# Relu² attention and a PReLU feed-forward on one core: two score chunks, not three, behind each A@V, and a second plain run of three under FFN1

## The chip, the cores and the metric

The kernel runs on one core of a Trainium2 chip. The metric is the device time of one execution in microseconds (us). The profile is that of one execution; its engines are PE (TensorE's matmuls), PEld (TensorE's weight loads), DVE (VectorE), ACT (ScalarE), POOL (GpSimd) and SP (SyncE, which here only issues DMAs).

## The reference

```python
# q, k, v: (8 batches, 12 heads, 448 tokens, 64), float32
scores = scale * np.matmul(q, k.transpose(0, 1, 3, 2))      # scale = 1/sqrt(64)
attn = np.maximum(scores, 0.0) ** 2 / S                      # S = 448
attn_out = np.matmul(attn, v)
x = attn_out.transpose(0, 2, 1, 3).reshape(B * S, H * D)     # 3584 x 768
h = x @ w_in                                                 # w_in: 768 x 2048
g = np.maximum(h, 0.0) + alpha * np.minimum(h, 0.0)          # alpha: 2048
out = g @ w_out                                              # w_out: 2048 x 768
```

## The kernel before

The matmuls run in bf16. Four heads of one batch make a *group*; there are 8 x 3 = 24 groups, n = 0 to 23. The 448 tokens are cut into 7 slices of 64 keys, j = 0 to 6. One (group, slice) is a *chunk*: `score_mm` gives it a pair of PSUM banks and four matmuls on 64x64 tiles of the array, `relu` takes it out of PSUM (on ScalarE for "A", on DVE for "D"), and `square` multiplies it with itself on DVE into an `at` tile. When all seven `at` tiles of a group are there, `attnv(n)` runs 28 matmuls on 64x64 tiles, and its result goes, half by ScalarE (line 205) and half by DVE (line 206), into `xT`, the input of the feed-forward.

FFN1 of a batch is 16 calls `f1(b, ff)`: six full-array matmuls into one bank, then `neg` on ScalarE (line 237) and the step that writes `gT` on DVE (line 238). FFN2 works on two batches together: `f2(sb, c, hf)` is 16 matmuls for 128 tokens and half of the columns, a copy `osb` on ScalarE (line 254) and two stores from SP's queue (line 260). After FFN1 of an even batch come 6 such units, after an odd one 8.

Attention of the next batches is woven into this by hand. The order in the source is the order on every engine (`manual_schedule`). The 126 chunks of groups 6 to 23 stand in one list, and `some(k)` takes the next k of it, with engines "ADA". `run(some(3))` is a *plain run*: three chunks' scores, relus and squares. `burst(n)` is a *burst*: three chunks' scores, `attnv(n)`, three more chunks' scores, then all six squares. Before: plain runs after three of the first FFN2 units, bursts 6, 7 and 8, and then in every batch from 2 to 6 one plain run before ff 8 and three bursts between the FFN2 units. That is 3 + 3 x 6 = 21 chunks a batch, as many as three groups have.

PSUM's eight banks are handed out at build time by age: `take_pair` gives the aligned pair whose younger use is oldest, `take_bank` the oldest bank. A matmul then waits until whoever last read that bank is done.

Groups from 6 on are transposed by DMA. `prepare(n)` calls `turn_dma(n)`: two DVE copies into `perm` (line 155) and one DMA transpose from SP's queue into a T tile (line 157, four buffers), which `score_mm` reads. It then has POOL load q, k and v of group n + 2 (lines 91 and 98), which takes buffers that the copies have freed. In a batch with n0 = 3(b + 1), `prepare(n0 + 2)` stands before ff 8, `prepare(n0 + 3)` before `burst(n0)` and `prepare(n0 + 4)` before `burst(n0 + 2)`. Other buffers that matter: `rl` 7, `at` 12, `neg` 3, `osb` 4.

Of the kernel before, what the change touches and what calls it, by code (L numbers as in the profile page):

```python
# [20 lines left out]
def kernel(  # L21
# [56 lines left out]
    def take_bank():  # L78
        i = min(range(8), key=lambda i: (taken[i], i))
        take(i, 1)  # L80
        return psum[:, i]
# [82 lines left out]
    def score_mm(n, j):  # L164
        ps = take_pair()
        t = T[n]
        for r in range(2):
            for c in range(2):
                nc.tensor.matmul(ps[64 * c:64 * c + 64, r, :S],  # L169
                                 t[64 * r:64 * r + 64, 1, j, 64 * c:64 * c + 64],  # L170
                                 t[64 * r:64 * r + 64, 0, :, 64 * c:64 * c + 64],
                                 start=True, stop=True)
        return ps

    def relu(ps, eng):
        rl = rl_pool.tile([128, 2, S], BF16, tag="rl", name="rl")
        if eng == "A":
            nc.scalar.activation(rl, ps[:, :, :S], ACTF.Relu)  # L178
        else:
            nc.vector.tensor_scalar(rl, ps[:, :, :S], 0.0, None, ALU.max)  # L180
        return rl
# [6 lines left out]
    def attnv(n):  # L188
        ps = take_pair()
        vv = vraw.pop(n)  # L190
        for j in range(NJ):
            a = att.pop((n, j))
            for r in range(2):
                for s in range(2):
                    nc.tensor.matmul(ps[64 * s:64 * s + 64, r, :S],  # L195
                                     vv[64 * r:64 * r + 64, s, j, :],
                                     a[64 * r:64 * r + 64, s],
                                     start=(j == 0), stop=(j == NJ - 1))
        b, g = divmod(n, NG)
        if g == 0:  # L200
            xT[b] = xT_pool.tile([128, NG, 2, S], BF16, tag="xT", name="xT")
        if n < 2:
            nc.scalar.activation(xT[b][:, g], ps[:, :, :S], ACTF.Copy, scale=out_scale)
            return
        nc.scalar.activation(xT[b][:, g, 0], ps[:, 0, :S], ACTF.Copy, scale=out_scale)  # L205
        nc.vector.tensor_scalar(xT[b][:, g, 1], ps[:, 1, :S], out_scale, None, ALU.mult)  # L206
# [3 lines left out]
    def sc(chunks):  # L210

        for n, j, eng in chunks:
            late.append((n, j, relu(score_mm(n, j), eng)))

    def sq(k=99):
        for g in late[:k]:
            square(*g)
        del late[:k]

    def run(chunks):  # L220
        sc(chunks)
        sq()
# [19 lines left out]
    def f1(b, ff):  # L242
        ps = take_bank()[:, :S]
        f1_mm(ps, b, ff, range(KM))
        f1_out(ps, b, ff)

    def f2(sb, c, hf, parts=((0, HALF),)):
        o = o_pool.tile([128, HALF], F32, tag="o", name="osb")
        for lo, hi in parts:
            ps = take_bank()[:, :hi - lo]  # L250
            for ff in range(KF):
                nc.tensor.matmul(ps, gT[sb][:, ff, bass.ts(c, 128)], w_out_sb[:, hf, ff, lo:hi],  # L252
                                 start=(ff == 0), stop=(ff == KF - 1))
            nc.scalar.copy(o[:, lo:hi], ps)  # L254
            for u in range(2):
                blk = 2 * c + u
                b, j = 2 * sb + blk // NJ, blk % NJ
                rows = out[b * S:(b + 1) * S].rearrange("(pp j) d -> j pp d", j=NJ)
                eng = nc.scalar if u and hi - lo < HALF else nc.sync
                eng.dma_start(out=rows[j][:, hf * HALF + lo:hf * HALF + hi], in_=o[64 * u:64 * u + 64, lo:hi])  # L260
# [57 lines left out]
    def prepare(n):  # L318
        if n < NQ:
            turn_dma(n)  # L320
        if n + 2 < NQ:
            load_qk(n + 2)
            load_v(n + 2)
# [38 lines left out]
    def some(k):  # L362
        lo = at_c[0]
        at_c[0] = min(lo + k, len(chunks))
        return [(n, j, e) for (n, j), e in zip(chunks[lo:at_c[0]], "ADA")]

    def burst(n):

        sc(some(3))
        attnv(n)  # L370
        sc(some(3))
        sq()

    early = []
# [19 lines left out]
    f2(0, 1, 1)  # L394
    run(some(3))
    f2(0, 2, 1)
    f2(0, 4, 0)
    prepare(9)
    burst(6)
    f2(0, 4, 1)  # L400
    f2(0, 5, 0)
    burst(7)
    f2(0, 5, 1)
    f2(0, 6, 0)
    prepare(10)
    burst(8)
    f2(0, 6, 1)

    for b in range(2, B):
        n0 = NG * (b + 1)  # L410
        last = b == B - 1
        sb = b // 2
        for ff in range(KF):
            if not last and ff == 8:
                run(some(3))
                prepare(n0 + 2)
            f1(b, ff)
        if b % 2 == 0:
            units = [(sb, c, h) for c in range(3) for h in range(2)]
            at = {1: 0, 3: 1, 5: 2}  # L420
        else:
            units = [(sb, c, h) for c in range(3, 7) for h in range(2)]
            at = {1: 0, 4: 1, 7: 2}
        for i, u in enumerate(units):
            if i in at and not last:
                g = at[i]
                if g != 1:
                    prepare(n0 + 3 + g // 2)
                burst(n0 + g)
            if last and i == len(units) - 1:  # L430
                f2(*u, parts=((0, 256), (256, HALF)))
            else:
                f2(*u)
# [30 lines left out]
```

## Time and profile before

| | |
|---|---|
| five runs, us | 393.89, 399.61, 392.79, 398.99, 401.05 |
| median, us | 398.99 |
| the profiled execution's own time, us | 394.08 |
| its span, us | 392.3 |
| PE busy | 379.0 us, 97% of the span |
| DVE busy | 263.6 us, 67% |
| ACT busy | 207.5 us, 53% |
| TensorE clock granted | full, in all slices |

The span is the time from the first to the last instruction of the program. Busy times are sums over instructions. PE's matmuls are pipelined and their ends are modelled, so lengths of PE's entries overlap what follows; the distance from one start to the next is the better measure. A time of a trace line is counted from the span's start.

| stage, from the trace | PE's time, us from the span's start |
|---|---|
| FFN1 of batch 2 | 125.18 to 144.14 |
| FFN2 units and bursts behind it | 144.14 to 168.16 |
| FFN1 of batch 3 | 168.16 to 187.11 |
| FFN2 units and bursts behind it | 187.11 to 216.50 |
| FFN1 of batch 4 | 216.50 to 235.46 |
| FFN1 of batch 7, the last | 349.56 to 367.72 |

### The profile page before, as it was taken

To read this page: it belongs to the slowest core of one execution; us is meant where nothing else is said; L and a number is where in the kernel's file an instruction comes from. 1 tells how busy PE (TensorE), PEld (TensorE's weight loads), DVE (VectorE), ACT (ScalarE), POOL (GpSimd) and SP (SyncE) were. 2 spreads that over 40 slices of the span, in tenths; PEclk is the share of its full clock that TensorE was granted. 3 is DMA by queue.
4 is the path that set the end of the run, shared out by engine and by line. 5 is a ranking of instruction groups with operands and counts; after the bars stand their busy time and mean duration, and the time that the engine had idled before them with its cause. 6 is when DMAs were issued, how large, how long until landed. Compare 5 with 4: busy or idle time off the path is not lost.

```text
span 392.3 us, 7956 instructions
## 1 busy us (share of the span) xinstructions
PE 379.0 (97%) x3228; PEld 215.7 (55%) x3228; DVE 263.6 (67%) x418; ACT 207.5 (53%) x332; POOL 65.6 (17%) x97
## 2 busy tenths in 40 slices
PE   6779999989999999999999999999999999999996
PEld 5434454535666456654666556655565546655564
DVE  3977965845678687878756688778756786735400
ACT  4966565524655546645545455565544556524311
POOL 7558112520202021202202022011100000000000
PEclk9999999999999999999999999999999999999999
DMA  9999999999677279482957339490842302120033
GB/s 177 191 204 203 206 211 201 139 149 194 99 122 124 56 119 165 77 116 31 170 118 135 64 41 173 105 144 15 143 96 49 89 10 60 42 60 2 11 72 81
DMA packets 71909, 43.75 MB, mean 112 GB/s; under 512 B 38208, under 2 KB 71872, under 8 KB 71872
## 3 DMA queue, kind: packets, MB, share of 16 engines
q0 software_dynamic: 27312, 23.04, 41.1%
q1 hardware_dynamic: 44128, 19.65, 25.3%
q8 instruction: 25, 0.41, 0.5%
q10 hardware_dynamic: 432, 0.56, 0.4%
q14 instruction: 12, 0.10, 0.1%
HBM read 47.00 MB, written 11.01 MB: 148 GB/s over the span
## 4 chain that ended last, share of the span: by engine, by line
PE 84%; DVE 6%; ACT 4%; DMA 4%; issue 1%; ACTq 0%; DVEq 0%
PE psum L252 37%; PE psum L229 32%; PE psum L169 7%; PE psum L195 6%; ACT rl L178 3%; DMA T<-perm 3%; DVE at L185 2%; DVE gT L238 1%; DMA qfirst<-in_q_dram 1%; DVE T L147 1%; DVE rl L180 1%; PE psum L144 1%; ACT xT L205 1%; DVE perm L155 0%; ACT osb L254 0%
## 5 line engine op out<-in xcount | busy, mean ns | idle before, releaser
L252 PE MATMUL psum<-w_out_sb,gT 128*128 128x384 bf16 (+2 forms) x912 | 151.8, 323 | 1.8 <-DVE gT L238 1.6
L229 PE MATMUL psum<-xT,w_in_sb 128*128 128x448 bf16 x768 | 148.7, 353 | 1.1 <-ACT xT L205 0.6
L252 PEld LDWEIGHTS <-gT 128*128 128x128 bf16 x912 | 87.6, 98 | 64.3 <-issue 6.7
L229 PEld LDWEIGHTS <-w_in_sb 128*128 128x128 bf16 x768 | 74.2, 98 | 71.8 <-issue 4.4
L238 DVE SCALAR_TENSOR_TENSOR gT<-neg,beta_sb,psum 128x448 bf16<-128x448 f32 x128 | 84.2, 679 | 39.9 <-ACT neg L237 39.5
L237 ACT ACTIVATE neg<-psum 128x448 f32<-128x448 f32 x128 | 69.3, 545 | 73.4 <-PE psum L229 63.5
L178 ACT ACTIVATE rl<-psum 128x896 bf16<-128x896 f32 x120 | 102.9, 928 | 1.2 <-PE psum L169 1.2
L185 DVE TENSOR_TENSOR at<-rl 128x896 bf16<-128x896 bf16 x168 | 94.1, 620 | 3.5 <-ACT rl L178 3.4
L254 ACT COPY osb<-psum 128x384 f32<-128x384 f32 (+2 forms) x57 | 27.0, 474 | 97.0 <-PE psum L252 91.5
L180 DVE TENSOR_SCALAR rl<-psum 128x896 bf16<-128x896 f32 x48 | 52.2, 1087 | 36.2 <-PE psum L169 36.2
L91 POOL DMA_DIRECT2D qraw<-in_q_dram x24 | 17.2, 719 | 193.0 <-DVE perm L155 172.2
L169 PE MATMUL psum<-T 64*64 64x448 bf16 x672 | 44.7, 355 | 3.6 <-ACT rl L178 1.3
L195 PE MATMUL psum<-at,vraw 64*64 64x448 bf16 x672 | 37.9, 351 | 0.7 <-DVE at L185 0.3
L169 PEld LDWEIGHTS <-T 64*64 64x64 bf16 x672 | 20.9, 105 | 21.2 <-issue 14.5
L195 PEld LDWEIGHTS <-vraw 64*64 64x64 bf16 x672 | 24.8, 106 | 11.0 <-issue 3.4
L206 DVE TENSOR_SCALAR xT<-psum 128x448 bf16<-128x448 f32 x22 | 13.7, 625 | 14.3 <-PE psum L195 7.2
L91 POOL DMA_DIRECT2D kraw<-in_k_dram x24 | 17.5, 728 | 7.2 <-DMA w_out_sb<-in_moe_w_out_dram 3.4
L98 POOL DMA_DIRECT2D vraw<-in_v_dram x25 | 18.2, 730 | 1.2 <-DMA w_in_sb<-in_moe_w_in_dram 0.3
L155 DVE COPY perm<-qraw 128x896 bf16<-128x896 bf16 x18 | 11.1, 615 | 5.7 <-DMA T<-perm 5.7
L205 ACT ACTIVATE xT<-psum 128x448 bf16<-128x448 f32 x22 | 12.0, 545 | 5.4 <-PE psum L195 5.4
L108 POOL DMA_DIRECT2D w_in_sb<-in_moe_w_in_dram x16 | 10.0, 627 | 7.8 <-DMA vraw<-in_v_dram 2.5
L155 DVE COPY perm<-kraw 128x896 bf16<-128x896 bf16 x18 | 11.0, 611 | 0.0
(19 smaller groups left out, 34.6 us busy)
## 6 DMA issues: line engine op xcount, KB each, us to landing
out_dram<-osb SPq DMA_DIRECT2D x110, 96.0 KB, 3.0
vraw<-in_v_dram POOLq DMA_DIRECT2D x25, 224.0 KB, 7.6
qraw<-in_q_dram POOLq DMA_DIRECT2D x24, 224.0 KB, 5.2
kraw<-in_k_dram POOLq DMA_DIRECT2D x24, 224.0 KB, 6.9
w_in_sb<-in_moe_w_in_dram POOLq DMA_DIRECT2D x16, 192.0 KB, 8.5
w_out_sb<-in_moe_w_out_dram POOLq DMA_DIRECT2D x2, 1536.0 KB, 18.9
qfirst<-in_q_dram SPq DMA_DIRECT2D x1, 448.0 KB, 4.5
kfirst<-in_k_dram ACTq DMA_DIRECT2D x1, 448.0 KB, 4.8
```

Of the source, the lines that this page charges most:

```text
L91: nc.gpsimd.dma_start(out=t.rearrange("p m j d -> p m (j d)"), in_=flat[:, 2 * g:2 * g + 2])
L155: nc.vector.tensor_copy(p[:, i], raw.pop((n, name)).rearrange("p s j d -> p j s d"))
L169: nc.tensor.matmul(ps[64 * c:64 * c + 64, r, :S], t[64 * r:64 * r + 64, 1, j, 64 * c:64 * c + 64], t[64 * r:64 * r + 64, 0, :, 64 * c:64 * ...
L178: nc.scalar.activation(rl, ps[:, :, :S], ACTF.Relu)
L180: nc.vector.tensor_scalar(rl, ps[:, :, :S], 0.0, None, ALU.max)
L185: nc.vector.tensor_tensor(a, rl, rl, ALU.mult)
L195: nc.tensor.matmul(ps[64 * s:64 * s + 64, r, :S], vv[64 * r:64 * r + 64, s, j, :], a[64 * r:64 * r + 64, s], start=(j == 0), stop=(j == NJ ...
L229: nc.tensor.matmul(ps, w_in_sb[:, km // 2, km % 2, bass.ts(ff, 128)], xT[b][:, km // 2, km % 2, :], start=(km == 0), stop=(km == KM - 1))
L237: nc.scalar.activation(neg, ps, ACTF.Relu, scale=-1.0)
L238: nc.vector.scalar_tensor_tensor(gT[b // 2][:, ff, (b % 2) * S:(b % 2) * S + S], neg, beta_sb[:, ff:ff + 1], ps, ALU.mult, ALU.add)
L252: nc.tensor.matmul(ps, gT[sb][:, ff, bass.ts(c, 128)], w_out_sb[:, hf, ff, lo:hi], start=(ff == 0), stop=(ff == KF - 1))
L254: nc.scalar.copy(o[:, lo:hi], ps)
```

## The change

The second part of a burst takes two chunks in place of three, so that its squares are five. A fourth plain run stands in the first FFN2 units, before `f2(0, 4, 0)`. In batches 2 to 6 the plain run before ff 8 is taken out, and one stands before ff 5 and another before ff 11; `prepare(n0 + 2)` stays before ff 8. A batch has 2 x 3 + 3 x 5 = 21 chunks again.

```diff
@@ def burst(n)
         sc(some(3))
         attnv(n)
-        sc(some(3))
+        sc(some(2))
         sq()
...
     f2(0, 1, 1)
     run(some(3))
     f2(0, 2, 1)
+    run(some(3))
     f2(0, 4, 0)
     prepare(9)
     burst(6)
...
         for ff in range(KF):
+            if not last and ff in (5, 11):
+                run(some(3))
             if not last and ff == 8:
-                run(some(3))
                 prepare(n0 + 2)
             f1(b, ff)
```

## The prediction

> **What bounds the kernel now.** I read the page first: busy times, then the chain that ended last.
>
> ```profile
> PE 379.0 (97%) x3228; PEld 215.7 (55%) x3228; DVE 263.6 (67%) x418; ACT 207.5 (53%) x332; POOL 65.6 (17%) x97
> PE 84%; DVE 6%; ACT 4%; DMA 4%; issue 1%; ACTq 0%; DVEq 0%
> ```
>
> TensorE is busy in 97% of the span and makes 84% of the chain. DVE and ScalarE have room on average. Next the waits of PE: all together they are under 10 us, and nearly all lie before 89 us. The change acts from 98 us on, so it can gain only what hides inside PE's busy time. I therefore took PE's timeline, in which each line gives start, length, engine and operation, and measured from start to start. First a burst of batch 4 (three score chunks, the A@V, three score chunks, then FFN2), with ScalarE's xT copy of its A@V:
>
> ```profile
> 238.16 0.76 PE L169 MATMUL psum<-T 64*64 64x448 bf16 x12
> 238.75 1.56 PE L195 MATMUL psum<-at,vraw 64*64 64x448 bf16 x28
> 240.07 0.80 PE L169 MATMUL psum<-T 64*64 64x448 bf16 x12
> 240.28 0.54 ACT L205 ACTIVATE xT<-psum 128x448 bf16<-128x448 f32 x1
> 240.87 5.36 PE L252 MATMUL psum<-w_out_sb,gT 128*128 128x384 bf16 x32
> ```
>
> The burst takes 240.87 - 238.16 = 2.71 us. Its last three chunks take 0.80 until FFN2 starts. ScalarE's xT copy ends at 240.82, 0.05 before FFN2's first matmul: FFN2 is handed the A@V's bank and waits for it. Now the plain run of batch 4 under FFN1, and FFN1 of the last batch, which has none:
>
> ```profile
> 225.68 0.76 PE L169 MATMUL psum<-T 64*64 64x448 bf16 x12
> 226.37 9.25 PE L229 MATMUL psum<-xT,w_in_sb 128*128 128x448 bf16 x48
> 349.56 18.32 PE L229 MATMUL psum<-xT,w_in_sb 128*128 128x448 bf16 x96
> 367.72 21.00 PE L252 MATMUL psum<-w_out_sb,gT 128*128 128x384 bf16 x144
> ```
>
> FFN1 without a run: 367.72 - 349.56 = 18.16, or 1.135 for each ff. FFN1 of batch 4, with the run, goes from 216.50 to FFN2's start at 235.46: 18.96.
>
> **What is added: six plain runs of three chunks.** One goes before f2(0, 4, 0); in batches 2 to 6 the run before ff 8 becomes two, before ff 5 and ff 11. A run costs PE 18.96 - 18.16 = 0.80 us. The runs between FFN2 units say the same: FFN2 starts at 95.12 and 98.52 with a unit of 2.60 and a run between, 0.80. Six cost 4.80 us. Three chunks of matmuls are some 3 x 0.19 = 0.57 of each 0.80 (0.19 is the difference between a score part of 8 matmuls, 57.46 to 57.86, and one of 12, 0.59); the other 0.23 is for entering and leaving 64x64 tiles.
>
> [...]
>
> **What is removed: a chunk of each burst.** 17 bursts have a second part now (groups 6 to 22). Each loses a chunk; group 22 loses two, since the list of 126 chunks runs out there. 16 + 2 = 18 chunks, the same as six runs. The trace has one burst of the new shape already, before batch 2:
>
> ```profile
> 57.86 1.49 PE L195 MATMUL psum<-at,vraw 64*64 64x448 bf16 x28
> 59.18 0.55 PE L169 MATMUL psum<-T 64*64 64x448 bf16 x8
> 59.66 2.77 PE L252 MATMUL psum<-w_out_sb,gT 128*128 128x384 bf16 x16
> ```
>
> Two chunks after the A@V: FFN2 starts 0.48 later, not 0.80. I followed the oldest-bank rule of take_pair and take_bank through the new order: FFN2 then gets the pair of the burst's third chunk, not the A@V's. That chunk's relu, ScalarE's second of the burst, ends 2.21 us after the burst's start (238.64 + 1.73), and FFN2 would start at 1.91 + 0.48 = 2.39, so the xT copy leaves PE's path with 0.18 to spare. 13 bursts save 0.80 - 0.48 = 0.32 each (4.16); the later two of batches 3 and 5 have 0.82 there and save 0.34 (4 x 0.34 = 1.36); group 22's second chunk is 0.19. Total 5.71. Bound from below: if FFN2 waited elsewhere, only the work would go, 18 x 0.19 = 3.4. I take 5.71, since the row has the same shape.
>
> **What moves between ScalarE and DVE.** some() gives its chunks "ADA", so a part of two is A, D: one relu per batch goes from ScalarE (0.93) to DVE (1.09). Neither is on the path in FFN2.
>
> **DVE under FFN1.** What hides the work there is this row: DVE after the run of batch 4.
>
> ```profile
> 226.96 1.08 DVE L180 TENSOR_SCALAR rl<-psum 128x896 bf16<-128x896 f32 x1
> 227.96 1.69 DVE L185 TENSOR_TENSOR at<-rl 128x896 bf16<-128x896 bf16 x3
> 229.56 0.61 DVE L155 COPY perm<-qraw 128x896 bf16<-128x896 bf16 x1
> 230.09 0.61 DVE L155 COPY perm<-kraw 128x896 bf16<-128x896 bf16 x1
> 230.62 3.04 DVE L238 SCALAR_TENSOR_TENSOR gT<-neg,beta_sb,psum 128x448 bf16<-128x448 f32 x5
> ```
>
> A run costs DVE 1.0 + 1.6, the two perm copies 1.1, a gT step 0.61 when queued and 0.68 when not. From the first run to FFN1's end PE takes 11 x 1.135 + 2 x 0.80 = 14.1 us; DVE has 11 x 0.61 to 0.68 + 2 x 2.6 + 1.1 = 13.0 to 13.8. It just fits. Step by step from the first run's start: squares end at 3.9, gT of ff 5, 6, 7 at 5.7, perm at 6.9, gT of 8, 9 at 8.0, gT of 10 at 8.9, then the second run's relu and squares to 11.6. The second run begins at 7.6; f1 of ff 11 begins at 8.3 in the bank of ff 9 (released at 8.0, 0.2 to spare with the semaphore); ff 12 at 9.4 in that of ff 10 (0.5 to spare). gT of 15 ends near 15.4, and FFN2's first unit needs it only in its last matmul, near 16.4. Cost taken: nothing. Without that cover, one gT step (0.65) too late costs about 0.5 per batch, 2.5 in five. In the new run before f2(0, 4, 0) DVE is tight as well: perm of prepare(9) ends about 1.0 after burst 6 begins, its D relu at 2.1, just when the second part asks for its bank at 2.10. Cost 0 to 0.1.
>
> **The T tiles.** The lead in chunks at a batch's start stays 27, but inside a batch chunks are taken earlier, so T is read sooner after its DMA transpose. SP's order is as before: the transpose stands behind the two stores of the unit ahead of the burst, which wait for ScalarE's osb copy. In the rows it issues 1.82 after its burst starts:
>
> ```profile
> 239.98 2.07 SPq L157 DMA_TRANSPOSE T<-perm  x1
> 255.99 3.06 SPq L157 DMA_TRANSPOSE T<-perm  x1
> DMA to landing us min/median/max: 3.5/7.7/14.5
> ```
>
> Asked one by one, the first lands after 7.7, the second after 9.2. Three cases. The T prepared ahead of a batch's first burst is now read by the last chunk of the next burst (chunk 42 is the first of group 12): in batches 2 and 4 at 8.01 - 0.32 + 2.10 = 9.79 after the first burst's start, against landings at 1.82 + 7.8 = 9.62 and 1.82 + 7.7 = 9.52; group 9 ahead of burst 6: 9.82 against 1.87 + 7.4. Margins 0.2 to 0.6. The T prepared ahead of the third burst is read by the second chunk of the ff 5 run: 2.39 + 2.60 + 5 x 1.135 + 0.10 + 0.19 = 10.96, against 1.82 + 9.2 = 11.02 after batches 2 and 4: 0.1 late each. Batches 3 and 5 have 10.7 us between bursts and landings of 3.6 to 7.7, so they are safe. The T prepared at ff 8 gains, because its perm no longer stands behind a run (about 1.6 earlier): over 1 to spare. POOL's loads follow their perm copies as before. I take 0.2 for all this.
>
> **Sum.** 4.80 - 5.71 + 0.2 = -0.7 us. The profiled execution took 394.08 (span 392.3 and 1.8 around it), so its like would be 393.4. The median of the runs shown is 398.99, 4.9 higher, in a spread from 392.79 to 401.05; on that footing I predict 398.3. About 2% is what a measurement of this kernel can tell from no change.
>
> **Rivals.**
>
> *T comes late (slower).* Place: last chunk of the second burst in batches 2 and 4 and of burst 7. If those transposes land after 9.2, as two neighbours do, each is read 11.0 - 9.8 = 1.2 before it lands: 3 x 1.2 = 3.6, and the sum is +2.7: 396.8 like the profile, 401.7 at the median. It decides once the three are 0.3 late on average, at landings of about 8.3. For: 9.2, 8.8 and 8.3 stand in the trace. Against: these three measured 7.4 to 7.8 in the same surroundings. Over 2% it takes landings like the 11.8 to 14.5 at 71 to 85 us, when DMA was crowded.
>
> *DVE becomes FFN1's bound.* 2.5 as above, sum +1.8: 395.9, or 400.8. For: 0.2 to spare, and at 85 to 88 us PE did step with DVE's gT, at 0.59 for each matmul. Against: DVE idles 0.46 in each ff with no run near, and makes that up.
>
> *The bursts give back only their work*, because FFN2 waits for the third chunk's relu instead: 4.80 - 3.4 + 0.2 = +1.6, 395.7 or 400.6. For: only 0.18 to spare. Against: the row at 59 us.
>
> *Clearly faster.* Over 2% is 8 us. All of the bursts' time beyond matmul work is 17 x (2.71 - 13 x 0.19) = 4 us, so nothing in the profile can give it; only a change in the spread of runs could.
>
> **How the numbers follow.** Forecast 0.60 (own range on the profile's footing 392 to 395); T late 0.17; DVE 0.09; work only 0.10; clearly faster 0.04. Of the T and DVE cases 0.10 is put beyond 2%. Same: 0.60 + 0.10 + 0.16 = 0.86. The range takes the low footing less a little, 391.8, up to T late at the median and a bit more, 402.5.
>
> **What would show it.** Right: FFN1 of batches 2 to 6 at 19.8 (+0.80); burst to FFN2 near 2.39 with an 8-matmul second part; the xT copy no longer just ahead of FFN2; PE with no new waits above 0.2. Wrong: PE waiting at L169 for T by DMA in second bursts or in the ff 5 run; PE waiting at L229 for gT after the second run; FFN2 starting 0.05 after a relu of ScalarE.

## The result, and the profile after

The changed kernel is slower: 1.0091 times the time before, 95% interval 1.0069 to 1.0113, some 3.6 us on 392. Its median over 46 runs is 398.87 (393.58 to 409.24). The kernel before, with 86 runs by then, has a median of 393.45 (391.13 to 401.88). Both spread for a reason of their own, taken up below: a wait of PE near 85 us that one trace shows and another does not. The ratio compares the runs within 1.5% of each kernel's fastest; the profiled execution of the changed kernel, 403.82 (span 402.1), is not among them, so its stages are compared with those of before, and its total is not.

The page's busy times and chain:

```profile
PE 384.9 (96%) x3228; PEld 213.7 (53%) x3228; DVE 267.5 (67%) x423; ACT 203.2 (51%) x327; POOL 65.6 (16%) x97
PE 83%; DMA 7%; DVE 5%; ACT 3%; issue 1%; ACTq 0%; DVEq 0%
```

PE's two longest waits (total us, times, longest):

```profile
PE psum L252 <- DVE gT L238: 2.9, 4, 2.1
PE psum L169 <- DMA T<-perm: 2.6, 1, 2.6
```

DMA's share of the chain is 7%, up from 4%, and PE has a wait that it did not have: 2.6 us, once, for a T tile. PE's timeline shows it in burst 7:

```profile
116.96 0.76 PE L169 MATMUL psum<-T 64*64 64x448 bf16 x12
117.55 1.56 PE L195 MATMUL psum<-at,vraw 64*64 64x448 bf16 x28
118.88 0.42 PE L169 MATMUL psum<-T 64*64 64x448 bf16 x4
121.90 0.38 PE L169 MATMUL psum<-T 64*64 64x448 bf16 x4 [2.60 <-DMA T<-perm]
122.22 7.05 PE L252 MATMUL psum<-w_out_sb,gT 128*128 128x384 bf16 x32
```

The last chunk of burst 7 is chunk 21, the first of group 9. Behind the wait, 32 FFN2 matmuls take 7.05 us where they take 5.37 at the full clock. The rest of the program did nearly what was forecast. Burst and FFN1 of batch 4:

```profile
225.62 5.84 PE L229 MATMUL psum<-xT,w_in_sb 128*128 128x448 bf16 x30
231.38 0.76 PE L169 MATMUL psum<-T 64*64 64x448 bf16 x12
232.08 6.99 PE L229 MATMUL psum<-xT,w_in_sb 128*128 128x448 bf16 x36
238.99 0.76 PE L169 MATMUL psum<-T 64*64 64x448 bf16 x12
239.69 5.85 PE L229 MATMUL psum<-xT,w_in_sb 128*128 128x448 bf16 x30
245.37 2.76 PE L252 MATMUL psum<-w_out_sb,gT 128*128 128x384 bf16 x16
248.06 0.76 PE L169 MATMUL psum<-T 64*64 64x448 bf16 x12
248.66 1.56 PE L195 MATMUL psum<-at,vraw 64*64 64x448 bf16 x28
249.98 0.61 PE L169 MATMUL psum<-T 64*64 64x448 bf16 x8
250.52 5.38 PE L252 MATMUL psum<-w_out_sb,gT 128*128 128x384 bf16 x32
```

FFN1 takes 245.37 - 225.62 = 19.75, 0.79 more than before; the burst takes 250.52 - 248.06 = 2.46, 0.25 less. Three bursts give back 0.75, nearly what the run costs.

Why group 9's tile was late stands in the engines' timeline. DVE's perm copies, POOL's loads that these copies release, and SP's transpose, first before, then after:

```profile
101.06 0.61 DVE L155 COPY perm<-qraw 128x896 bf16<-128x896 bf16 x1
101.59 0.61 DVE L155 COPY perm<-kraw 128x896 bf16<-128x896 bf16 x1
101.97 0.72 POOL L91 DMA_DIRECT2D qraw<-in_q_dram  x1 [15.48 <-DVE perm L155]
105.69 3.83 SPq L157 DMA_TRANSPOSE T<-perm  x1
```

```profile
108.99 0.61 DVE L155 COPY perm<-qraw 128x896 bf16<-128x896 bf16 x1
109.52 0.61 DVE L155 COPY perm<-kraw 128x896 bf16<-128x896 bf16 x1
109.91 0.72 POOL L91 DMA_DIRECT2D qraw<-in_q_dram  x1 [21.44 <-DVE perm L155]
111.02 3.23 SPq L157 DMA_TRANSPOSE T<-perm  x1
```

That transpose alone, from issue to landing:

```profile
DMA to landing us min/median/max: 10.8/10.8/10.8
```

Before, the loads (672 KB for q, k and v) started 3.7 us ahead of the transpose, which landed 7.4 after its issue. After, the fourth plain run keeps DVE busy until just ahead of burst 6, the perm copies come 2.6 us later against burst 6 (they start 0.2 before it, 108.99 to 109.16, where before it was 2.8, 101.06 to 103.82), and the loads start 1.1 us ahead of the transpose, which is issued as long after the burst's start as before (1.86 against 1.87). It lands after 10.8.

### The profile page after: what moved, and what is told of

The parts are those of the page before. It is cut to its first block, busy times and chain, and to the rows that moved or that the text cites. A ratio compares the mean times of both kernels' runs of the same rounds, so it can differ in the third digit from the quotient of the medians.

```text
span 402.1 us, 7931 instructions
## 1 busy us (share of the span) xinstructions
PE 384.9 (96%) x3228; PEld 213.7 (53%) x3228; DVE 267.5 (67%) x423; ACT 203.2 (51%) x327; POOL 65.6 (16%) x97
## 4 chain that ended last, share of the span: by engine, by line
PE 83%; DMA 7%; DVE 5%; ACT 3%; issue 1%; ACTq 0%; DVEq 0%
PE psum L252 36%; PE psum L229 32%; PE psum L169 8%; PE psum L195 7%; DMA T<-perm 6%; ACT rl L178 2%; DVE at L185 2%; DVE gT L238 1%; DMA qfirst<-in_q_dram 1%; DVE T L147 1%; PE psum L144 1%; DVE rl L180 1%; DVE perm L155 0%; ACT neg L237 0%; ACT osb L254 0%
## 5 line engine op out<-in xcount | busy, mean ns | idle before, releaser
L252 PE MATMUL psum<-w_out_sb,gT 128*128 128x384 bf16 (+2 forms) x912 | 156.2, 329 | 3.0 <-DVE gT L238 2.9
L178 ACT ACTIVATE rl<-psum 128x896 bf16<-128x896 f32 x115 | 99.5, 928 | 1.5 <-PE psum L169 1.4
L180 DVE TENSOR_SCALAR rl<-psum 128x896 bf16<-128x896 f32 x53 | 57.6, 1087 | 44.7 <-PE psum L169 44.7
L169 PE MATMUL psum<-T 64*64 64x448 bf16 x672 | 46.9, 360 | 6.7 <-DMA T<-perm 2.6
L169 PEld LDWEIGHTS <-T 64*64 64x64 bf16 x672 | 18.4, 106 | 26.8 <-issue 17.0
```

The source lines that it names most:

```text
L169: nc.tensor.matmul(ps[64 * c:64 * c + 64, r, :S], t[64 * r:64 * r + 64, 1, j, 64 * c:64 * c + 64], t[64 * r:64 * r + 64, 0, :, 64 * c:64 * ...
```

## The experiments

**The head of the change alone**: the fourth run and two-chunk bursts 6 to 8; the batches as before. The edit of the kernel before:

```diff
-    def burst(n):
+    def burst(n, second=3):
...
-        sc(some(3))
+        sc(some(second))
...
     f2(0, 2, 1)
+    run(some(3))
     f2(0, 4, 0)
     prepare(9)
-    burst(6)
+    burst(6, 2)        # 7 and 8 in the same way
```

> Only the head of the change: the fourth plain run before f2(0, 4, 0) and two-chunk second parts in bursts 6, 7 and 8; batches 2 to 6 as before. Theory (T of group 9 comes late): the loss is all here. The last chunk of burst 7 waits some 1 to 3 us for group 9's DMA transpose, which lands over 10 us after its issue, and FFN2 behind it runs partly at a lower clock: 2 to 4 us slower than before (ratio 1.005 to 1.010), as much as the whole change. Rival (the splitting of the batches costs it: twelve changes of tiling mode, DVE under FFN1): this kernel is within 0.5 us of before, since one run and three smaller bursts come to 0.80 - 3 x 0.25 = 0.05.

Ratio 1.0105 (1.0066 to 1.0145): as much as the whole change, and just above the range expected. The wait stands at the same place, with the transpose landing after 10.8 again:

```profile
112.97 0.42 PE L169 MATMUL psum<-T 64*64 64x448 bf16 x4
116.00 0.38 PE L169 MATMUL psum<-T 64*64 64x448 bf16 x4 [2.61 <-DMA T<-perm]
116.31 5.37 PE L252 MATMUL psum<-w_out_sb,gT 128*128 128x384 bf16 x32
```

Here FFN2 behind the wait runs at its usual 5.37; the lower clock that was expected with it did not come.

**The batches' part alone**: runs before ff 5 and ff 11 and two-chunk bursts from batch 2 on; the head as before. The edit of the changed kernel, in which `burst` now takes the size of its second part:

```diff
     f2(0, 2, 1)
-    run(some(3))
     f2(0, 4, 0)
     prepare(9)
-    burst(6)
+    burst(6, 3)        # 7 and 8 in the same way
```

> Only the batches' part of the change: runs before ff 5 and ff 11, two-chunk second parts in the bursts of batches 2 to 6; the head as before, bursts 6 to 8 with three. Theory (T of group 9 comes late): five runs cost 4.0 and fourteen bursts give back some 10 x 0.25 + 4 x 0.32 + 0.19 = 4.0, plus one wait of 0.4 for T in the ff 5 run of batch 5: within 1 us of before (ratio 0.999 to 1.003), no wait for T at burst 7. Rival (the batches cost it): 2.5 to 4 us slower, ratio 1.006 to 1.010.

The profiled run has a span of 390.1 and no wait for T or gT. It took 391.87 and is the fastest of six; the best of before on that chip is 391.35. The other five took 397.8 to 401.45, as 9 of the 25 runs of before beside them did (397.39 to 401.38); why it was five of six here is not shown. The one clean run fits the theory; the comparison by itself is inconclusive. That the loss lies in the head rests on the experiment ahead of this one.

**prepare(9) ahead of the fourth run.**

```diff
     f2(0, 2, 1)
+    prepare(9)
     run(some(3))
     f2(0, 4, 0)
-    prepare(9)
     burst(6)
```

> The changed kernel with one call moved: prepare(9) stands ahead of the fourth plain run, not behind f2(0, 4, 0), so group 9's perm copies and its DMA transpose come some 4 us sooner. Theory (T of group 9 comes late): PE has no wait for T in burst 7, no lower clock behind it; the kernel is 2.5 to 4 us faster than the changed kernel and within 1 us of before (ratio 0.998 to 1.003). Rival (the wait for T is only in the one profile, and the loss lies in the batches): no gain over the changed kernel, ratio 1.007 to 1.011 to before.

No wait for T, span 389.9, best 391.69. The ratio is 1.0044 (1.0001 to 1.0087), half of the loss and above the 1.003 expected: the spread is still there. The transpose lands after 10.7 here too, with the loads again 1.1 us ahead of it. It is just issued sooner, 9.3 us before burst 7 (100.42 to 109.76) in place of 5.9, and lands 0.7 before chunk 21 reads it.

**POOL's loads held back**, with the transpose where the changed kernel has it:

```diff
+    gate_sb = singles.tile([128, 1], F32)
...
             nc.scalar.copy(o[:, lo:hi], ps)
+            if (sb, c, hf) == (0, 4, 1):
+                nc.gpsimd.tensor_copy(gate_sb, o[:, 0:1])
```

> The changed kernel, with POOL's next loads (q, k, v of group 12, which wait only for group 9's perm copies) held back by a one-column POOL copy of the osb tile of f2(0, 4, 1), some 4 us later. The transpose of group 9 is issued where it was. Theory (its landing grew from 7.4 to 10.8 because the perm copies moved to 1.5 us ahead of the transpose and the loads with them): landing 4 to 6 us, no wait at burst 7, time as with prepare(9) moved, within 1 us of before. Rival (the transpose is slow for its stores or by chance): landing stays at 9 to 11, the wait stays, ratio 1.007 to 1.011.

The loads start at 108.41, 4.5 us after the transpose at 103.9, and the same transpose lands in less than half the time. Its landing, then burst 7, now without a gap in its second part:

```profile
DMA to landing us min/median/max: 5.0/5.0/5.0
```

```profile
111.79 0.61 PE L170 MATMUL psum<-T 64*64 64x448 bf16 x8
```

With nothing but the loads moved, the landing went from 10.8 to 5.0 and the wait went: the loads made that transpose late. The ratio is 1.0046 (1.0011 to 1.0081), again above what was expected, with a wait of 0.8 left: for the T of group 12, in the second burst of batch 2.

**One chunk moved**: burst 7's second part takes one chunk, burst 8's three, by the same argument of `burst`.

```diff
-    burst(7)
+    burst(7, 1)
...
-    burst(8)
+    burst(8, 3)
```

> The changed kernel with one chunk moved: burst 7's second part takes one chunk and burst 8's three, so chunk 21, the first of group 9, is read some 8 us later. Everything else, group 9's transpose and its slow landing too, stays as in the changed kernel. Theory (the loss is PE's wait for that one T tile): no wait for T at burst 7 and 2 to 4 us faster than the changed kernel, at best level within 0.7 us of before (ratio 0.998 to 1.005), although the transpose still lands 10 to 11 us after its issue. Rival (slow landings as such, or DMA traffic, cost it): still 1.007 to 1.011.

Burst 7 has no wait, although the transpose lands after 11.4: ratio 1.0022 (0.9989 to 1.0056). Its best time, 392.94, is 1.8 above before, more than the 0.7 expected. The profiled run (395.4) has the next margin that failed, group 12's tile (landing 9.7) in batch 2's second burst:

```profile
156.84 0.42 PE L169 MATMUL psum<-T 64*64 64x448 bf16 x4
158.72 0.38 PE L169 MATMUL psum<-T 64*64 64x448 bf16 x4 [1.45 <-DMA T<-perm]
```

Another 2.1 us of that run lie ahead of the change: its first FFN1 matmul starts at 25.0, where the kernel before has 22.9, and PE had waited 1.3 there for early loads of q and k. What holds the faster runs of this kernel above before is not shown by a trace.

**The spread.** In the changed kernel's profile PE stands near 85 us behind DVE, which stands behind a transpose:

```profile
85.41 0.62 DVE L155 COPY perm<-qraw 128x896 bf16<-128x896 bf16 x1 [7.46 <-DMA T<-perm]
87.19 0.34 PE L252 MATMUL psum<-w_out_sb,gT 128*128 128x384 bf16 x1 [2.10 <-DVE gT L238]
```

perm has two buffers, so prepare(8)'s copies wait until group 6's transpose has landed (11.8 in the profile before, 13.6 here), and the gT steps behind them on DVE wait too. Group 8 happens to be loaded twice in both kernels, at line 347 and in prepare(6), just ahead of those transposes. Five kernels leave the second load out:

```diff
     def prepare(n):
...
-        if n + 2 < NQ:
+        if n + 2 < NQ and n != 6:
             load_qk(n + 2)
             load_v(n + 2)
```

The kernel before with that edit:

> The kernel before, without the second load of group 8: q, k and v of group 8 are loaded at line 347 and once more in prepare(6), just ahead of the three DMA transposes of FFN1 of batch 1; the second load (672 KB) is left out. Theory (the spread of both kernels comes from PE waiting near 85 us for gT behind perm copies that wait for the transposes of group 6, which land late in crowded DMA): fewer or no runs at 394 and above, best level the same 391.4 or a little lower, ratio to before 0.985 to 0.998. Rival (the spread has another source, or the other loads crowd it as much): the same spread, ratio 0.998 to 1.002.

All 11 runs lie between 391.15 and 391.64, against 391.11 to 399.13 for before beside it; the ratio is 0.9983 (0.996 to 1.0006), the median 391.37. Group 6's transpose lands after 6.5. The spread went with the second load. The changed kernel with that edit:

> The changed kernel without the second load of group 8, so that its own cost is read without the wait near 85 us that both kernels have in some runs. Theory (T late at burst 7, and small T waits in batches 2 to 5): 2.0 to 4.5 us above 391.4, every run, with a wait of 2 to 3 us for T at burst 7. Rival (the loss is tied to the wait near 85 us, which the change makes more frequent): level of before, 391.2 to 392.

394.51 to 397.72, ratio 1.0118 (1.0088 to 1.0148), with 2.3 us of waiting for T in burst 7 in the profile. That is 3.1 to 6.3 above 391.4, where 2.0 to 4.5 was expected. This is the change's own cost with the other disturbance away: the medians of the two kernels with one load are 396.04 and 391.37, 4.7 apart, though on two chips. The profiled runs, 394.51 and 391.17, are 3.3 apart: 2.55 is the lateness of burst 7's last chunk, about 0.3 a late T in the ff 5 run of batch 5, 0.25 the changed order itself (the last experiment). With prepare(9) moved, and with the one chunk moved:

> The changed kernel with prepare(9) ahead of the fourth run and without the second load of group 8. Theory: both waits (burst 7's T, gT near 85 us) are gone: runs close together, best level 391.4 to 392.0, median below that of before. Rival: spread as before, 391.7 to 399.

> The changed kernel with burst 7 at one and burst 8 at three chunks in the second part, and without the second load of group 8. Theory: as the kernel with prepare(9) ahead and one load: runs close together at 391.4 to 392.2. Rival: spread as before, 391.7 to 399.

The first: 391.48 to 393.24, ratio 1.0003 (0.9972 to 1.0034); the profiled run waits 1.0 for group 12's tile in batch 2, which landed after 9.2. The second: 391.48 to 395.42, ratio 1.0031 (1.0004 to 1.0059). Both ratios are to the kernel before with its spread; against the kernel before with one load, run beside them (median 391.37), the medians are 1.0 and 1.9 us higher (392.35 and 393.30). Both kernels were also expected closer together. In the first, the thin margin in batch 2 is in the trace; in the second, the profiled run is the fastest of all and has no such wait, so what its longer runs waited for is not shown. The last kernel gives every T more time. Besides one load and prepare(9) ahead of the fourth run it has:

```diff
         for i, u in enumerate(units):
+            if i + 1 in at and not last and at[i + 1] != 1:
+                prepare(n0 + 3 + at[i + 1] // 2)
             if i in at and not last:
-                g = at[i]
-                if g != 1:
-                    prepare(n0 + 3 + g // 2)
-                burst(n0 + g)
+                burst(n0 + at[i])
```

> The changed kernel without the second load of group 8, with prepare(9) ahead of the fourth run and, in batches 2 to 6, the two prepare calls ahead of bursts moved one FFN2 unit earlier, so that each DMA transpose is issued about 2 to 3 us sooner relative to the chunk that reads it. Theory (the steady part of the change is worth nothing either way, 6 x 0.80 against 4.7 given back by the bursts, and all of the loss is waits for T): no wait of PE for T anywhere, runs within 0.5 us of each other at 391.0 to 391.8, ratio to before 0.996 to 1.000. Rival (the extra runs cost something of their own): 392.5 or more with no T wait in the trace.

No wait for T anywhere; 391.46 to 392.68 with eleven of twelve runs within 0.42; ratio 0.9987 (0.9961 to 1.0013); median 391.72, against 391.37, on another chip, for the kernel before with one load. So with no tile late, the rest of the loss is gone too. It shows what the changed order is worth by itself. From FFN2's start behind the third plain run to the start of the last batch's FFN2, in the kernel before with one load and then in this one:

```profile
95.66 1.64 PE L252 MATMUL psum<-w_out_sb,gT 128*128 128x384 bf16 x9
...
364.85 5.36 PE L252 MATMUL psum<-w_out_sb,gT 128*128 128x384 bf16 x32
```

```profile
96.03 1.15 PE L252 MATMUL psum<-w_out_sb,gT 128*128 128x384 bf16 x6
...
365.47 4.71 PE L252 MATMUL psum<-w_out_sb,gT 128*128 128x384 bf16 x28
```

269.19 and 269.44: the changed order costs 0.25 us when nothing waits.

## Why the prediction was wrong

**The runs' price was right.** FFN1 rose by 0.79 (0.80 said), and DVE held up nothing under FFN1: PE shows no wait for gT after the second run. Whatever going to 64x64 tiles and back costs (the changes of tiling mode of the first experiment's rival) is inside the 0.23 taken from the rows; no run shows it alone.

**The bursts' saving was mis-sized.** 0.32 was said for the ordinary burst and 0.34 for the later ones of batches 3 and 5; they gave 0.25 (2.71 to 2.46) and 0.32 (2.78 to 2.46, 2.83 to 2.51). The xT copy did leave PE's path, as forecast: in batch 4's burst it now ends after FFN2's start at 250.52.

```profile
250.19 0.54 ACT L205 ACTIVATE xT<-psum 128x448 bf16<-128x448 f32 x1
```

But little had been lost to it: 12 score matmuls take 0.80 until FFN2 in a burst and 0.70 in a plain run (97.82 to 98.52), so the wait was 0.1 at most. FFN2's start now comes 0.55 after the second part's, where the row at 59 us had 0.48; why it is not 0.48 is not shown. FFN2 does not wait for the third chunk's relu, which ends at 250.28. The steady sum is 4.8 - (13 x 0.25 + 4 x 0.32 + 0.19) = 0.1, and 0.25 by the last experiment, in place of -0.9.

**The step that failed is the landing of group 9's tile.** The prediction had the right chunk, in the right burst, with the right margin for a landing of 7.4 (9.82 against 1.87 + 7.4), and it had the perm copies ending 1.0 after burst 6 begins (110.13 - 109.16 = 0.97 in the trace). It charged that delay to DVE alone and let "POOL's loads follow their perm copies as before" stand as reassurance, when following them was the harm: the loads moved onto the transpose, and 7.4 became 10.8. The term of 0.2 for all T tiles should have held this one wait: by the prediction's own sum 1.87 + 10.8 - 9.82 = 2.85 late; the chunk's matmuls start 121.90 - 118.88 - 0.19 = 2.83 late (the wait's 2.60 is counted from the modelled end of the chunk ahead). The clause "in the same surroundings" in the rival is where it broke. Of the 3.6 to 4.7 us lost in place of 0.7 gained, this tile explains the most, and the bursts about 1.

**The rival "T comes late" is what happened.** It named burst 7 and batches 2 and 4, and priced each at 1.2 with landings of 9.2. Burst 7 waited 2.3 to 2.6 in each of the three traces that left its tile and loads as the change has them (the changed kernel, its head alone, and with one load), and in the first the slower matmuls behind the wait cost 1.7 more, which the rival had not priced. Batch 2's second burst waited 0.8 to 1.45 in three experiments and not in the changed kernel's own profile (landing 7.8). The ff 5 run of batch 5 was put 0.1 late; in the changed kernel its second chunk starts 0.65 after the first, in place of 0.19, at a landing of 9.6. In batch 3, put 0.1 late as well, it came in time (landing 8.9). Batch 4's second burst waited in none of the traces.

**The footing.** The median of five runs, 398.99, was taken as the level. 86 runs put it at 393.45, with a lowest of 391.13: three of the five lay near 400, in the upper cluster. That the forecast of 398.3 comes within 0.6 of the measured median, 398.87, is luck: a footing 5.5 too high and a change of the wrong sign cancel. The trace had shown that wait (1.6 us of PE behind gT), and it was passed over as lying ahead of the change.

## What to carry to other kernels

A transfer's duration is not a constant to be copied from the trace of before (here 7.4 became 10.8): list what starts within a few us of it, and if the edit moves any of these, price the overlap from rows with the same distances. When an edit reads a buffer earlier, work out the margin of each reader, and take a margin of a few tenths as a wait, since the next run's landings will differ by more than that (group 12's tile in batch 2 landed after 7.8 us in one trace and after 9.7 in another). When runs of one kernel spread in clusters, look for a wait that is in one trace and not in another before taking a median as the footing.

## What the runs showed of the hardware

**A transpose beside loads.** One DMA transpose of the same 448 KB (all traces, from 100 us on) landed after 3.4 to 5.3 us near the program's end, where no loads start close to it, and after 5.0 with the loads held back. With the first of the three loads 4.1 to 4.9 us ahead it was 5.0 to 7.0; with 3.5 to 3.7, 7.3 to 8.0; with 1.9 to 2.4, 7.1 to 9.9; with 1.1, 9.8 to 11.4. It is no rule of the distance alone: with the first load 0.3 ahead, as at ff 8, 53 landings took 6.4 to 9.7, more than half of them at most 7.0. What the loads did to group 9's tile, the experiment that held them back shows: it landed after 5.0 in place of 10.8. Why 1.1 us is so much worse than 0.3 these runs don't tell: at 1.1 two of the three loads and SP's stores stand ahead of the transpose, at ff 8 one load and no stores.

**TensorE's clock after a wait.** The granted clock by stretches (us, busy times, clock, DMA share, GB/s), the changed kernel first and the head alone second:

```profile
120.00:124.00 4.00, 2.10 (x12) 1.12 (x13) 1.66 (x3) 0.44 (x1) 0.00 (x0) 0.86 0.48 113
124.00:128.00 4.00, 4.00 (x20) 2.07 (x18) 3.16 (x6) 0.48 (x1) 1.07 (x2) 0.71 0.00 0
```

```profile
112.00:116.00 4.00, 1.39 (x31) 0.92 (x22) 1.39 (x2) 2.52 (x4) 0.00 (x0) 1.00 0.95 175
116.00:120.00 4.00, 4.00 (x27) 2.38 (x28) 3.57 (x6) 0.48 (x1) 0.00 (x0) 1.00 0.01 3
```

The same wait of 2.6 us was followed by a clock of 0.71 and 1.7 us of slower matmuls in one run, and by a clock of 1.00 and 32 matmuls in the usual 5.37 us in the other. In the first profile the wait of 2.10 us near 85 us was followed by a lower clock too, 0.50 from 90 to 94 us. Why the two runs differ is not shown. What they do show is that a wait of 2.6 us cost its own length in one run and 1.7 us more than that in the other.
